# The second MLP pair with one tile per PSUM bank, two operand splits moved into the last w_in step, and even token groups

## The chip, the cores and the metric

The kernel runs on one core of one Trainium2 chip. The metric is the device time of one launch in microseconds (us), as the median of several runs. The profile comes from one further execution, taken with the hardware profiler; stretches below are given in us from that execution's first instruction.

## The reference

Linear attention per head, normalised by its root mean square, feeds two MLP pairs, all in float32:

```python
kv  = einsum('bhsd,bhse->bhde', k, v)             # 8 batches, 8 heads, 576 tokens, head size 64
out = einsum('bhsd,bhde->bhse', q, kv)
x   = out / sqrt(mean(out * out) + 1e-6) * g_norm  # turned to 4608 tokens x 512
x   = (sigmoid(x @ w_gate) * (x @ w_val)) @ w_out  # first pair, inner width 1536
h   = x @ w_in                                     # second pair, 512 -> 2048
g   = where(h >= 1, h, where(h <= -1, 0, (h + 1)**2 / 4))
y   = g @ w_out                                    # 2048 -> 512
```

The change touches the last three lines alone: the second pair.

## The kernel before, in words

Every float32 operand of a matmul is split into a high part, rounded to the type that the matrix engine takes (`fp32r`), and a low part, the remainder; a product is then three matmuls: high by high, high by low, low by high. ACT copies the high part and DVE subtracts to get the low one.

The second pair (`class Second`, from line 712) computes both matrix products with Winograd's form of Strassen's scheme: 2 x 2 blocks, seven products in place of eight, with sums taken before and after. The columns of a matmul are tokens. The 4608 tokens are cut into five groups. A group holds two halves of `n2` tokens each, with `n2` from `SIZES` (512, 512, 512, 384, 384), so that each matmul is 128 x 128 by `n2` columns.

A group has two stages, written out by hand in one function, `group` (line 810); each engine runs its own instructions in the order in which that function issues them.

- **w_in.** Eight steps `s`. A step forms seven products, each of six matmuls (`product`, line 774, matmuls on line 778), and so 42 matmuls. They go to four PSUM banks: `A` takes a11, later s2 and s3 on top; `D` takes a12; `B` takes s1, later s4 on top; `C` takes a22. Between the products ACT copies the state of a bank to SBUF (`p[:, 0]`, `p[:, 1]`, `u[:, 0]`, `u[:, 1]`, tiles named `kept`), and DVE adds bank and copy into the four quarters `q` of a tile `G[k]` (named `g`, two steps to a tile). Even steps use banks 0 to 3, odd steps 4 to 7. The activation `g` of the reference is a chain for two quarters at a time (`chain`, line 817): ACT relu (line 822), ACT square (line 825), DVE min and max (line 828). It runs a step late, as `late[0]` to `late[5]`, between the next step's copies and adds.
- **w_out.** 28 pieces `m`, seven products by four tiles `G[k]`, 12 matmuls each (line 910). A piece takes an operand that `split` (line 836) makes: ACT copies its high part, DVE the low part, into a tile named `gh` of the pool `gsp`, which has three buffers and which the tiles `r` of the chain share. `split(m + 2)` is issued ahead of the matmuls of piece `m`. After every fourth piece a result is copied out of a bank by ACT or added by DVE and, when complete, stored.

The weights of a step (`wst`, 1792 KB) and of an out product (`wo`, 2048 KB) come by DMA from DRAM on the SP queue, each with two buffers. SP runs its DMAs in order, a wait included.

Banks are allocated in pairs: `banks` (line 787) gives a tile of two banks, `A` and `D` are the halves of one such tile, `B` and `C` those of another. In w_out a result of two column blocks (`o` = 0, 1) fills the two halves of one tile. The tile framework keeps order by whole tiles: an instruction that writes a tile waits for those that read it, whichever half they touch.

Just ahead of the second pair, `store` (line 591) copies the first pair's last result out of PSUM to four SBUF tiles `ev` and sends them to DRAM by POOL's queue. The pools of the second pair take over the first pair's SBUF; a tile there waits until what lay in its place is done.

Of the kernel before, what the change touches and what calls it, by code (L numbers as in the profile page):

```python
# [7 lines left out]
F32 = mybir.dt.float32  # L8
# [3 lines left out]
ALU = mybir.AluOpType  # L12
# [2 lines left out]
NT, DM, FF1, FF2 = B * S, H * D, 1536, 2048  # L15
P = 128
T = 512
SIZES = (512, 512, 512, 384, 384)
NB = NT // T
NP = H // 2  # L20
KC = DM // P
# [12 lines left out]
def attn_gated_mlp_kernel(ctx: ExitStack, tc: tile.TileContext, a: dict, out: bass.AP):  # L34
# [33 lines left out]
    def act_copy(o, i):  # L68
        nc.scalar.activation(out=o, in_=i, func=AF.Copy)  # L69
# [4 lines left out]
    def split(src, hi, lo):  # L74

        act_copy(hi, src)
        nc.vector.tensor_tensor(out=lo, in0=src, in1=hi.bitcast(F32), op=ALU.subtract)  # L77
        return hi, lo
# [626 lines left out]
    class Second:  # L705
# [13 lines left out]
        def tt(self, o, x, y, op):  # L719
            nc.vector.tensor_tensor(out=o, in0=x, in1=y, op=op)  # L720
# [63 lines left out]
            t = self.wo2[i] = self.wo2p.tile([P, HF, 2, 2 * P], F32R, name="wo2", tag="wo2")  # L784
            nc.sync.dma_start(out=t.bitcast(F32), in_=wo2d[d][:, at])

        def banks(self, n):
            pool = (self.chain_p, self.acc_p)[n // 2]
            return pool.tile([P, 2, T], F32, name=f"bank{n}", tag=f"bank{n % 2}")[:, :, :self.n]

        def kept(self):
            return self.sv.tile([P, 2, T], F32, name="kept", tag="kept")[:, :, :self.n]
# [18 lines left out]
        def group(self, g, more):  # L811
# [25 lines left out]
            def split(m):  # L837
                i, k = divmod(m, HF // 2)
                src = G[k][:, self.OUT[i][1]]
                o = ops[m] = self.gsp.tile([P, 2, 2, T], F32R, name="gh2", tag="gsp")[:, :, :, :n2]  # L840
                act_copy(o[:, 0], src)
                tt(o[:, 1], src, o[:, 0].bitcast(F32), ALU.subtract)

            late = ()
            for s in range(HF):
                X, Y = (self.banks(s % 2 * 2 + e) for e in range(2))
                A, D, B, C = X[:, 0], X[:, 1], Y[:, 0], Y[:, 1]
                q = [G[s // 2][:, i, s % 2] for i in range(4)]
                self.ws = self.w_next
                if s + 1 < HF:  # L850
                    self.w_next = self.w_load(s + 1) if s else self.w_after
                elif more:
                    x = self.x_load(g + 1)
                if s in (2, 4):
                    self.wo2_load(s // 2 - 1)
                p, u = self.kept(), self.kept()
                r = self.gsp.tile([P, 4, T], F32, name="r", tag="gsp")[:, :, :n2]
                this = chain(s, 0, r[:, 0:2]) + chain(s, 2, r[:, 2:4])
                self.product(A, "a11", "b11")
                act_copy(p[:, 0], A)  # L860
                self.product(D, "a12", "b21")
                if late:
                    late[1]()
                tt(q[0], D, p[:, 0], ALU.add)
                self.product(B, "s1", "t1")
                act_copy(p[:, 1], B)
                if late:
                    late[3]()
                    late[2]()
                self.product(A, "s2", "t2", False)  # L870
                act_copy(u[:, 0], A)
                if late:
                    late[4]()
                self.product(C, "a22", "t4")
                if late:
                    late[5]()
                self.product(B, "s4", "b22", False)
                tt(q[1], B, u[:, 0], ALU.add)
                this[0]()
                if s and s % 2 == 0:  # L880
                    t1(s // 2 - 1)
                self.product(A, "s3", "t3", False)
                act_copy(u[:, 1], A)
                tt(q[2], A, p[:, 1], ALU.add)
                tt(q[3], C, u[:, 1], ALU.add)
                late = this
# [1 line left out]
            late[1]()  # L888
            late[3]()
            late[2]()  # L890
            split(0)
            late[4]()
            late[5]()
            split(1)
            t1(HF // 2 - 1)
            A, E, D, C = (self.banks(n) for n in range(4))
            bank = (A, E, A, D, E, A, C)
            if more:
                steps = self.x_steps(x)
# [5 lines left out]
            def matmuls(m, o):  # L905
                i, k = divmod(m, HF // 2)
                for e in range(2):
                    for n, (h, l) in enumerate(((0, 0), (0, 1), (1, 0))):
                        first = k == e == n == 0 and i in (0, 1, 3, 6)
                        nc.tensor.matmul(bank[i][:, o], self.wo2[i][:, 2 * k + e, h, o * P:(o + 1) * P], ops[m][:, l, e],  # L910
                                         start=first, stop=k == HF // 2 - 1 and e == 1 and n == 2, skip_group_check=True)

            for m in range(last + 1):
                i, k = divmod(m, HF // 2)
                if m + 2 <= last:
                    split(m + 2)
                if 2 <= m < 6:
                    tt(G[m - 2][:, 1], G[m - 2][:, 2], G[m - 2][:, 1], ALU.subtract)
                if 8 <= m < 12:
                    tt(G[m - 8][:, 0], G[m - 8][:, 1], G[m - 8][:, 0], ALU.subtract)  # L920
                if 12 <= m < 16:
                    tt(G[m - 12][:, 3], G[m - 12][:, 3], G[m - 12][:, 1], ALU.subtract)
                if more and (m in (0, 1, 6, 7) or 16 <= m < 24):
                    run(steps, 1)
                if more and m == 24:
                    self.w_after = self.w_load(1)
                if k == 0 and i + 1 < 7 and i:
                    self.wo2_load(i + 1)
                for o in range(2):
                    matmuls(m, o)  # L930
                    if m == last:
                        tt(u3[:, o], C[:, o], u3[:, o], ALU.add)
                        goes(1, 0, u3, slice(o, o + 1))
                if k == HF // 2 - 1:
                    if i == 0:
                        p1 = self.kept()
                        act_copy(p1, A)
                    elif i == 1:
                        p5 = self.kept()
                        act_copy(p5, E)  # L940
                    elif i == 2:
                        u2 = self.kept()
                        act_copy(u2, A)
                    elif i == 3:
                        tt(p1, D, p1, ALU.add)
                        goes(0, 0, p1)
                    elif i == 4:
                        tt(u2, E, u2, ALU.add)
                        goes(0, 1, u2)
                    elif i == 5:  # L950
                        u3 = self.kept()
                        act_copy(u3, A)
                        tt(p5, A, p5, ALU.add)
                        goes(1, 1, p5)


    with tc.manual_schedule():
# [368 lines left out]
        for k, j in enumerate(pairs):  # L1326
# [73 lines left out]
            if more:  # L1400
                run(steps)
                store(j + 1, norm_tags)
            else:
                run(second.xsteps)
                store(j + 1, ("nm", "nr", "nt", "wol"))
        first_part.close()
        second.rest()

# [39 lines left out]
```

## Time and profile before

| what | value |
|---|---|
| median of 3 runs | 1752.38 us (1751.16 to 1753.39) |
| the profiled execution | 1749.95 us, of which its span is 1748.0 us |
| granted TensorE clock, mean of the span | 0.984 |
| PE busy, share of the span | 95% |
| ACT, DVE busy | 52%, 67% |
| second pair, first to last matmul | from 952.4 us to about 1744.4 us |

Busy time of PE is the union of its matmuls' durations. A matmul's duration covers its way through the array, so that the next one starts well before it ends; the time per matmul is the distance from one start to the next. "Idle before" and the name behind the arrow say how long an engine had nothing to do and which instruction's end let it go on. PEclk is the granted share of the clock: 1.0 is 2.4 GHz, 0.5 is 1.2 GHz. In a table by stage the engines stand in the order PE, PEld (weight loads), DVE, ACT, POOL, each with its number of instructions in brackets.

### The profile page before, as it was taken

The numbers are of one execution on the slowest core, as the hardware profiler recorded it, in microseconds if no ns is written. First come the engines' busy times: TensorE is split into PE (matmuls) and PEld (weight loads), VectorE is DVE, ScalarE is ACT, GpSimd is POOL, SyncE is SP. The second block draws the span as 40 slices with busy tenths as digits, with TensorE's granted clock in tenths as the row PEclk, the third lists the DMA queues.
The fourth block names the chain that finished last, engine by engine and source line by source line (L and its number), as shares of the span: only waits on it lengthen the run. The fifth ranks groups of instructions, "written<-read, shape, count | busy, mean of one in ns | idle before, by whom it ended". The sixth has DMA issues, their size and how long they took to land.

```text
span 1748.0 us, 22357 instructions
## 1 busy us (share of the span) xinstructions
PE 1667.2 (95%) x8132; PEld 1378.3 (79%) x8132; DVE 1178.1 (67%) x1734; ACT 914.8 (52%) x1336; POOL 186.0 (11%) x292
## 2 busy tenths in 40 slices
PE   9999999999999999999998989998999899989888
PEld 6778887888878877888786767776877688888888
DVE  6888747768667678768745458745855685575565
ACT  4453445456477577544433565456536654553553
POOL 1212122323200111112211000000000000000000
PEclk8999999999999999999999999999999999999999
DMA  9776776677757778699855464555357445755825
GB/s 295 241 243 230 244 256 222 211 250 255 241 172 250 261 232 280 202 370 357 299 171 200 181 237 161 193 223 217 145 187 270 157 169 205 307 187 210 320 112 194
DMA packets 123678, 400.02 MB, mean 229 GB/s; under 512 B 15657, under 2 KB 22953, under 8 KB 113969
## 3 DMA queue, kind: packets, MB, share of 16 engines
q1 hardware_dynamic: 102640, 331.48, 54.7%
q0 software_dynamic: 20928, 67.13, 10.3%
q8 instruction: 64, 1.05, 0.2%
q14 instruction: 46, 0.37, 0.1%
HBM read 315.18 MB, written 83.36 MB: 228 GB/s over the span
## 4 chain that ended last, share of the span: by engine, by line
PE 79%; issue 7%; DMA 5%; ACT 4%; DVE 4%; POOL 1%; SPq 0%; POOLq 0%; DVEq 0%; ACTq 0%
PE bank L910 19%; PE bank L778 16%; PE h L94 6%; PE h L95 6%; PE h L96 6%; PE acc L94 5%; PE acc L95 4%; PE acc L96 4%; PE pA L648 4%; PE pE L648 3%; DMA wst<-w2d 2%; ACT kept L69 2%; DMA wo<-wo2d 1%; ACT r L822 1%; PE kvps L159 1%
## 5 line engine op out<-in xcount | busy, mean ns | idle before, releaser
L910 PE MATMUL bank<-gh,wo 128*128 128x512 f32 (+1 forms) x1680 | 363.6, 377 | 33.0 <-ACT gh L69 21.9
L910 PEld LDWEIGHTS bank<-gh,wo 128*128 128x128 f32 x1680 | 314.7, 194 | 81.9 <-ACT gh L69 27.3
L69 ACT ACTIVATE gh<-g 128x1024 fp32r<-128x1024 f32 (+2 forms) x164 | 151.4, 923 | 158.6 <-PE bank L910 132.2
L778 PE MATMUL bank<-x_t,wst 128*128 128x512 f32 (+1 forms) x960 | 210.8, 368 | 0.0
L778 PE MATMUL bank<-x_b,wst 128*128 128x512 f32 (+1 forms) x720 | 174.1, 377 | 35.6 <-ACT kept L69 33.2
L720 DVE TENSOR_TENSOR gh<-g,gh 128x1024 fp32r<-128x1024 f32 (+1 forms) x140 | 156.2, 1116 | 55.8 <-ACT gh L69 54.7
L778 PEld LDWEIGHTS bank<-x_t,wst 128*128 128x128 f32 x960 | 175.9, 188 | 22.7
L69 ACT ACTIVATE kept<-bank 128x512 f32<-128x512 f32 (+3 forms) x180 | 106.4, 591 | 166.7 <-PE bank L778 131.5
L720 DVE TENSOR_TENSOR g<-bank,kept 128x512 f32<-128x512 f32 (+1 forms) x160 | 98.1, 634 | 135.9 <-PE bank L778 87.0
L778 PEld LDWEIGHTS bank<-x_b,wst 128*128 128x128 f32 x720 | 129.4, 189 | 68.3 <-ACT kept L69 48.5
L94 PE MATMUL acc<-gh,woh 128*128 128x512 f32 x420 | 164.8, 392 | 0.0
L95 PE MATMUL acc<-gl,woh 128*128 128x512 f32 x420 | 163.8, 390 | 0.3 <-DVE gl L77 0.3
L94 PE MATMUL h<-xh,w 128*128 128x512 f32 x384 | 151.6, 395 | 0.0
L95 PE MATMUL h<-xl,w 128*128 128x512 f32 x384 | 149.7, 390 | 0.2 <-DVE xl L84 0.2
L96 PE MATMUL h<-xh,w 128*128 128x512 f32 x384 | 149.5, 389 | 0.0
L828 DVE SCALAR_TENSOR_TENSOR g<-r,g 128x1024 f32<-128x1024 f32 (+1 forms) x80 | 89.1, 1114 | 82.2 <-ACT r L825 82.2
L96 PE MATMUL acc<-gh,woh 128*128 128x512 f32 x324 | 126.2, 389 | 0.0
L822 ACT ACTIVATE r<-g,half 128x1024 f32<-128x1024 f32 (+1 forms) x80 | 85.0, 1062 | 76.0 <-DVE g L720 76.0
L648 PE MATMUL pA<-xc,wc 128*128 128x512 f32 x432 | 111.1, 393 | 3.1 <-ACT u L69 3.0
L648 PEld LDWEIGHTS pA<-xc,wc 128*128 128x128 f32 x432 | 81.3, 189 | 21.2 <-ACT u L69 4.3
L94 PEld LDWEIGHTS acc<-gh,woh 128*128 128x128 f32 x420 | 78.8, 188 | 18.7 <-issue 1.2
L95 PEld LDWEIGHTS acc<-gl,woh 128*128 128x128 f32 x420 | 78.8, 188 | 17.2 <-DVE gl L77 1.1
(193 smaller groups left out, 2655.2 us busy)
## 6 DMA issues: line engine op xcount, KB each, us to landing
wst<-w2d SPq DMA_DIRECT2D x40, 1792.0 KB, 7.5
wo<-wo2d SPq DMA_DIRECT2D x35, 2048.0 KB, 8.1
wc<-w1d SPq DMA_DIRECT2D x168, 256.0 KB, 5.4
woh<-wo1d SPq DMA_DIRECT2D x162, 256.0 KB, 4.8
raw<-in_w SPq DMA_DIRECT2D x32, 512.0 KB, 5.7
raw<-in_w_gv SPq DMA_DIRECT2D x24, 512.0 KB, 5.5
w1d<-w2half POOLq DMA_DIRECT2D x48, 256.0 KB, 4.2
w2d<-w2half POOLq DMA_DIRECT2D x48, 256.0 KB, 4.8
```

Source lines behind the costliest of these rows:

```text
L69: nc.scalar.activation(out=o, in_=i, func=AF.Copy)
L94: nc.tensor.matmul(ps, w[0][:, wsl], x[0], start=first, stop=False)
L95: nc.tensor.matmul(ps, w[0][:, wsl], x[1], start=False, stop=False)
L96: nc.tensor.matmul(ps, w[1][:, wsl], x[0], start=False, stop=last)
L159: nc.tensor.matmul(ps[g * D:(g + 1) * D, e], k[:, s], v[:, s], start=c == 0, stop=c == NSC)
L648: nc.tensor.matmul(o, w[:, h, sl], x[c][l], start=first and c == n == 0, stop=c == 1 and n == 2, skip_group_check=True)
L720: nc.vector.tensor_tensor(out=o, in0=x, in1=y, op=op)
L778: nc.tensor.matmul(bank, self.ws[w][h][:, sl], self.xo[x][:, l, c], start=first and c == n == 0, stop=c == 1 and n == 2, skip_group_check= ...
L822: nc.scalar.activation(out=r, in_=v, func=AF.Relu, bias=self.half, scale=0.5)
L828: nc.vector.scalar_tensor_tensor(out=v, in0=r, scalar=1.0, in1=v, op0=ALU.min, op1=ALU.max)
L910: nc.tensor.matmul(bank[i][:, o], self.wo2[i][:, 2 * k + e, h, o * P:(o + 1) * P], ops[m][:, l, e], start=first, stop=k == HF // 2 - 1 and ...
```

## The change

Five edits, all for the second pair.

1. `SIZES` becomes (464, 464, 464, 464, 448). The number of matmuls and the sum of their columns stay what they were.
2. `bank` replaces `banks`: eight tiles of one bank each.
3. In the last w_in step, `split(0)` is issued behind `late[4]` and `split(1)` behind the relu `this[0]`; they were issued behind the step, between `late[2]`, `late[4]` and `late[5]`.
4. In w_out a result that was copied by one ACT instruction over two banks, or added by one DVE instruction, takes two, one per bank (`keep`, `result`).
5. The first pair's last `store` takes its four `ev` tiles from the pool of the weights (`wo`) in place of four tiles of the pool of temporaries.

```diff
-SIZES = (512, 512, 512, 384, 384)
+SIZES = (464, 464, 464, 464, 448)
...
-        def banks(self, n):
-            pool = (self.chain_p, self.acc_p)[n // 2]
-            return pool.tile([P, 2, T], F32, name=f"bank{n}", tag=f"bank{n % 2}")[:, :, :self.n]
+        def bank(self, n):
+            pool = (self.chain_p, self.acc_p)[n // 4]
+            return pool.tile([P, T], F32, name=f"bank{n}", tag=f"bank{n % 4}")[:, :self.n]
...
-                X, Y = (self.banks(s % 2 * 2 + e) for e in range(2))
-                A, D, B, C = X[:, 0], X[:, 1], Y[:, 0], Y[:, 1]
+                A, D, B, C = (self.bank(s % 2 * 4 + e) for e in range(4))
...
                 if late:
                     late[4]()
+                if s == HF - 1:
+                    split(0)
                 self.product(C, "a22", "t4")
...
                 this[0]()
+                if s == HF - 1:
+                    split(1)
...
             late[2]()
-            split(0)
             late[4]()
             late[5]()
-            split(1)
             t1(HF // 2 - 1)
-            A, E, D, C = (self.banks(n) for n in range(4))
+            A, E, D, C = ([self.bank(n + o) for o in range(2)] for n in (0, 2, 4, 6))
...
+            def keep(b):
+                t = self.kept()
+                for o in range(2):
+                    act_copy(t[:, o], b[o])
+                return t
+
+            def result(h, e, b, t):
+                for o in range(2):
+                    tt(t[:, o], b[o], t[:, o], ALU.add)
+                goes(h, e, t)
...
                     if m == last:
-                        tt(u3[:, o], C[:, o], u3[:, o], ALU.add)
+                        tt(u3[:, o], C[o], u3[:, o], ALU.add)
...
                 run(second.xsteps)
-                store(j + 1, ("nm", "nr", "nt", "wol"))
+                store(j + 1, None)
```

How the instructions move is read from the built programs. First PE, the third w_in step of the first group; a row is an instruction, out<-in, columns, and the semaphores that it waits for (`Activation` is ACT). `x_b_9359` is the operand of the product into `D`. Before:

```order
L778 MATMUL bank_9696<-x_b_9323,wst 128x512 [waits DMAHW5_49]
L778 MATMUL bank_9696<-x_b_9323,wst 128x512 x5
L778 MATMUL bank_9696<-x_b_9359,wst 128x512 [waits Activation_49]
L778 MATMUL bank_9696<-x_b_9359,wst 128x512 x5
L778 MATMUL bank_9697<-x_t_9382,wst 128x512 x6
L778 MATMUL bank_9696<-x_t_9424,wst 128x512 [waits DVE_49]
L778 MATMUL bank_9696<-x_t_9424,wst 128x512 x5
L778 MATMUL bank_9697<-x_t_9460,wst 128x512 [waits Activation_49]
L778 MATMUL bank_9697<-x_t_9460,wst 128x512 x5
L778 MATMUL bank_9697<-x_b_9479,wst 128x512 x6
L778 MATMUL bank_9696<-x_t_9513,wst 128x512 [waits Activation_49]
L778 MATMUL bank_9696<-x_t_9513,wst 128x512 x5
```

and now:

```order
L778 MATMUL bank_9700<-x_b_9323,wst 128x464 [waits DMAHW5_49,DVE_49]
L778 MATMUL bank_9700<-x_b_9323,wst 128x464 x5
L778 MATMUL bank_9701<-x_b_9359,wst 128x464 x6
L778 MATMUL bank_9702<-x_t_9382,wst 128x464 x6
L778 MATMUL bank_9700<-x_t_9424,wst 128x464 [waits Activation_49]
L778 MATMUL bank_9700<-x_t_9424,wst 128x464 x5
L778 MATMUL bank_9703<-x_t_9460,wst 128x464 [waits DVE_49]
L778 MATMUL bank_9703<-x_t_9460,wst 128x464 x5
L778 MATMUL bank_9702<-x_b_9479,wst 128x464 [waits Activation_49]
L778 MATMUL bank_9702<-x_b_9479,wst 128x464 x5
L778 MATMUL bank_9700<-x_t_9513,wst 128x464 [waits Activation_49]
L778 MATMUL bank_9700<-x_t_9513,wst 128x464 x5
```

The first matmul into `D` (operand `x_b_9359`) waited for ACT, which reads `A`; now it waits for nothing, and the waits that are left stand where a product is added on top of a bank.

Second ACT, from the last w_in step of the first group into w_out. `r<-g` is the relu, `r<-r` the square, `kept<-bank` the copy of a bank, `gh_...<-g_...` the high part of a split. Before:

```order
L69 ACTIVATE kept<-bank_10018 128x512 [waits DVE_49,PE_49]
L825 ACTIVATE r<-r 128x1024 [waits Activation_49]
L822 ACTIVATE r<-g_9576,half_9571 128x1024 [waits DVE_49]
L69 ACTIVATE kept<-bank_10018 128x512 [waits PE_49]
L825 ACTIVATE r<-r 128x1024 [waits Activation_49]
L822 ACTIVATE r<-g_9576,half_9571 128x1024 [waits DVE_49]
L69 ACTIVATE gh_10087<-g_9573 128x1024
L825 ACTIVATE r<-r 128x1024 [waits Activation_49]
L69 ACTIVATE gh_10092<-g_9574 128x1024
L69 ACTIVATE gh_10102<-g_9575 128x1024 [waits DVE_49]
```

and now:

```order
L69 ACTIVATE kept<-bank_10032 128x464 [waits PE_49]
L825 ACTIVATE r<-r 128x2x464 [waits Activation_49]
L69 ACTIVATE gh_10078<-g_9573 128x2x464
L822 ACTIVATE r<-g_9576,half_9571 128x2x464 [waits DVE_49]
L69 ACTIVATE gh_10096<-g_9574 128x2x464 [waits Activation_49]
L69 ACTIVATE kept<-bank_10032 128x464 [waits PE_49]
L825 ACTIVATE r<-r 128x2x464 [waits Activation_49]
L822 ACTIVATE r<-g_9576,half_9571 128x2x464 [waits DVE_49]
L825 ACTIVATE r<-r 128x2x464 [waits Activation_49]
L69 ACTIVATE gh_10124<-g_9575 128x2x464 [waits PE_49]
L69 ACTIVATE x_b_10127<-xin 128x2x464 [waits DMAHW6_49,DMAHW5_49]
L69 ACTIVATE gh_10142<-g_9576 128x2x464 [waits DVE_49,PE_49]
```

The first two `gh` copies have moved up: the first stands ahead of the last step's first relu, the second ahead of its last copy of a bank. The third `gh` copy now waits for PE, because the buffer that it gets is the first one's.

Third DVE at the same place. `g<-bank,kept` adds a bank and its copy, `g<-r,g` is the min and max, `gh<-g,gh` the low part of a split. Before:

```order
L828 SCALAR_TENSOR_TENSOR g_9576<-r,g_9576 128x2x512 [waits DVE_49,Activation_49] x2
L720 TENSOR_TENSOR g_9576<-bank_10019,kept 128x512 [waits PE_49]
L720 TENSOR_TENSOR g_9576<-bank_10018,kept 128x512 [waits Activation_49]
L720 TENSOR_TENSOR g_9576<-bank_10019,kept 128x512
L828 SCALAR_TENSOR_TENSOR g_9576<-r,g_9576 128x2x512 [waits DVE_49,Activation_49]
L720 TENSOR_TENSOR gh_10087<-g_9573,gh_10087 128x1024 [waits Activation_49]
L828 SCALAR_TENSOR_TENSOR g_9576<-r,g_9576 128x2x512 [waits DVE_49,Activation_49]
L720 TENSOR_TENSOR gh_10092<-g_9574,gh_10092 128x1024 [waits DMASW6_49,DMASW7_49,DMASW5_49,Activation_49]
L720 TENSOR_TENSOR g_9576<-g_9576 128x1024 [waits DVE_49]
L720 TENSOR_TENSOR gh_10102<-g_9575,gh_10102 128x1024 [waits DMASW1_49,DMASW2_49,DMASW0_49,Activation_49]
```

and now:

```order
L720 TENSOR_TENSOR g_9576<-bank_10033,kept 128x464 [waits PE_49,Activation_49]
L828 SCALAR_TENSOR_TENSOR g_9576<-r,g_9576 128x2x464 [waits DVE_49,Activation_49]
L720 TENSOR_TENSOR gh_10078<-g_9573,gh_10078 128x2x464 [waits Activation_49]
L828 SCALAR_TENSOR_TENSOR g_9576<-r,g_9576 128x2x464 [waits DVE_49]
L720 TENSOR_TENSOR g_9576<-bank_10034,kept 128x464 [waits PE_49]
L720 TENSOR_TENSOR gh_10096<-g_9574,gh_10096 128x2x464 [waits DMASW6_49,DMASW5_49,DMASW7_49,DVE_49,Activation_49]
L720 TENSOR_TENSOR g_9576<-bank_10032,kept 128x464 [waits Activation_49]
L720 TENSOR_TENSOR g_9576<-bank_10035,kept 128x464
L828 SCALAR_TENSOR_TENSOR g_9576<-r,g_9576 128x2x464 [waits DVE_49,Activation_49] x2
L720 TENSOR_TENSOR g_9576<-g_9576 128x2x464 [waits DVE_49]
L720 TENSOR_TENSOR gh_10124<-g_9575,gh_10124 128x2x464 [waits Activation_49]
```

The first low part now stands ahead of a min and max and of the add `g<-bank_10034`, and the second ahead of the last two adds.

## Rows read from the trace of the kernel before

**Rows 1.** Busy time by stage: stretch and length, then engines' busy us, PEclk, DMA share, GB/s

```profile
952.40:1045.20 92.80, 80.03 (x337) 63.32 (x335) 40.16 (x49) 46.56 (x61) 2.26 (x5) 0.96 0.60 218
...
1131.10:1215.20 84.10, 78.56 (x337) 62.28 (x336) 40.06 (x48) 45.78 (x60) 0.00 (x0) 1.00 0.57 210
1215.20:1220.10 4.90, 0.21 (x1) 0.00 (x0) 2.44 (x4) 4.49 (x6) 0.00 (x0) 0.74 0.76 255
1220.10:1300.00 79.90, 78.64 (x337) 64.18 (x338) 66.05 (x57) 39.99 (x39) 0.00 (x0) 0.97 0.49 185
...
1470.00:1537.40 67.40, 61.52 (x337) 57.86 (x335) 31.52 (x48) 36.31 (x60) 0.00 (x0) 1.00 0.66 254
...
1541.40:1607.80 66.40, 62.49 (x337) 61.05 (x338) 51.16 (x57) 31.54 (x39) 0.00 (x0) 0.95 0.59 220
```

**Rows 2.** Who PE waited for, 952 to 1748 us: total us, times, longest

```profile
PE bank L778 <- ACT kept L69: 33.2, 40, 8.0
PE bank L910 <- ACT gh L69: 21.9, 5, 4.7
PE bank L910 <- DMA wo<-wo2d: 4.7, 5, 1.5
PE bank L910 <- DVE kept L720: 3.7, 5, 0.8
...
PE bank L778 <- DMA wst<-w2d: 2.4, 4, 0.9
```

**Rows 3.** Timeline, a w_in step at 512 columns: start us, length us, engine, instruction

```profile
1164.30 0.60 ACT L69 ACTIVATE kept<-bank 128x512 f32<-128x512 f32 x1 [0.20 <-PE bank L778]
...
1164.95 1.65 PE L778 MATMUL bank<-x_b,wst 128*128 128x512 f32 x6 [0.69 <-ACT kept L69]
...
1166.45 4.24 PE L778 MATMUL bank<-x_t,wst 128*128 128x512 f32 x18
...
1170.53 1.52 PE L778 MATMUL bank<-x_b,wst 128*128 128x512 f32 x6
```

**Rows 4.** Timeline, PE alone, a w_in step at 384 columns

```profile
1500.90 1.20 PE L778 MATMUL bank<-x_b,wst 128*128 128x384 f32 x6
1501.94 1.21 PE L778 MATMUL bank<-x_t,wst 128*128 128x384 f32 x6
```

**Rows 5.** Timeline, the first w_in step of all

```profile
961.24 0.60 ACT L69 ACTIVATE kept<-bank 128x512 f32<-128x512 f32 x1 [8.04 <-DMA x2d<-ev]
...
961.89 2.93 PE L778 MATMUL bank<-x_b,wst 128*128 128x512 f32 x6 [7.97 <-ACT kept L69]
```

**Rows 6.** Timeline, the handover from w_in to w_out, second group

```profile
1214.97 1.15 ACT L822 ACTIVATE r<-g,half 128x1024 f32<-128x1024 f32 x1 [1.90 <-DVE g L720]
...
1216.03 0.58 ACT L69 ACTIVATE kept<-bank 128x512 f32<-128x512 f32 x1
...
1216.64 1.29 DVE L720 TENSOR_TENSOR g<-bank,kept 128x512 f32<-128x512 f32 x2 [1.70 <-ACT kept L69]
...
1217.96 1.15 ACT L822 ACTIVATE r<-g,half 128x1024 f32<-128x1024 f32 x1 [0.41 <-DVE g L720]
1219.02 1.04 ACT L69 ACTIVATE gh<-g 128x1024 fp32r<-128x1024 f32 x1
...
1220.09 1.23 DVE L720 TENSOR_TENSOR gh<-g,gh 128x1024 fp32r<-128x1024 f32 x1 [1.03 <-ACT gh L69]
...
1220.11 0.79 PE L910 MATMUL bank<-gh,wo 128*128 128x512 f32 x1 [4.70 <-ACT gh L69]
...
1221.37 23.88 PE L910 MATMUL bank<-gh,wo 128*128 128x512 f32 x98 [0.47 <-DVE gh L720]
```

**Rows 7.** Instruction groups by shape, PE, line 186: busy us, mean ns

```profile
L186 PE MATMUL X<-qraw,kvw 64*64 64x512 f32 x16 | 4.1, 614 | 0.1
...
L186 PE MATMUL X<-qraw,kvw 64*64 64x448 f32 x16 | 2.9, 562 | 0.0
```

**Rows 8.** DMA issues, 1494 to 1503 us: size, us from issue to landing

```profile
wst<-w2d SPq DMA_DIRECT2D x1, 1792.0 KB, 9.1
```

More of the change, by code (lines that the diff above doesn't have):

```diff
@@ L909, in matmuls @@
                         first = k == e == n == 0 and i in (0, 1, 3, 6)
-                        nc.tensor.matmul(bank[i][:, o], self.wo2[i][:, 2 * k + e, h, o * P:(o + 1) * P], ops[m][:, l, e],
+                        nc.tensor.matmul(bank[i][o], self.wo2[i][:, 2 * k + e, h, o * P:(o + 1) * P], ops[m][:, l, e],
                                          start=first, stop=k == HF // 2 - 1 and e == 1 and n == 2, skip_group_check=True)
+            def keep(b):
[7 more added lines that the diff above has]
+                goes(h, e, t)
             for m in range(last + 1):
@@ L935, in group @@
                     if i == 0:
-                        p1 = self.kept()
-                        act_copy(p1, A)
+                        p1 = keep(A)
                     elif i == 1:
-                        p5 = self.kept()
-                        act_copy(p5, E)
+                        p5 = keep(E)
                     elif i == 2:
-                        u2 = self.kept()
-                        act_copy(u2, A)
+                        u2 = keep(A)
                     elif i == 3:
-                        tt(p1, D, p1, ALU.add)
-                        goes(0, 0, p1)
+                        result(0, 0, D, p1)
                     elif i == 4:
-                        tt(u2, E, u2, ALU.add)
-                        goes(0, 1, u2)
+                        result(0, 1, E, u2)
                     elif i == 5:
[L951 to L954, printed above, removed]
+                        u3 = keep(A)
+                        result(1, 1, A, p5)
     with tc.manual_schedule():
```

## The prediction

> **What bounds the kernel now.** The first view to read is busy time by stage [rows 1]: it gives how long each stage of the second pair takes, which is to be held against its matmuls alone. The price of a matmul is in the timelines. At 512 columns 18 of them run from 1166.45 to 1170.53 [rows 3], 0.2267 us each; at 384 columns six run from 1500.90 to 1501.94 [rows 4], 0.1733 us each. The difference, 0.0533 us for 128 columns, is 2.4 columns per ns. A stage has 336 matmuls: 76.2 us at 512, 58.2 us at 384. Six wide stages and four narrow ones are 690 us; from 952.4 to about 1744.4 the second pair takes 792. So 102 us are not matmul time, and they are what the change can touch. [Rows 1] place them: a wide w_in takes 84.1 (7.9 over), its handover to w_out 4.9, its w_out 79.9 (3.7 over). A narrow w_in is 9.2 over, a narrow w_out 8.2. The first w_in takes 92.8, 8.7 more than the second.
>
> Who is waited for is the second view [rows 2]: 40 waits for the ACT copy `kept`, one a step; five for ACT's `gh`, one a handover; then DMAs and DVE.
>
> **The waits in w_in.** [Rows 3] show the 40 waits: ACT copies bank A at 1164.30, and the product into bank D starts at 1164.95, after 0.69 us idle. The copy reads A, the product writes D; they share a tile. With what the restart costs, a wide step loses 7.9 / 8 = 0.99 us, a narrow one a little less. The order of the changed program has no wait on that product. What is late next: the product on top of A waits for the same copy, but two products later, 2.5 us, and the copy takes 0.6 us. ACT's work in a step, four copies, two relus and two squares (0.6 and about 1.1 us, [rows 6]), is under 7 us of the 8.7 that a step will take, and DVE's less. So I take this wait as gone at full: nothing else in the step is late by the rows.
>
> The first step's wait is another one [rows 5]: `kept` lies where the last `ev` tiles lay, and its copy stands 8.04 us until their DMA has landed; PE stands 7.97. With `ev` in the weights' pool that place is under `wo`, which is first loaded two steps later. I keep 0.5 us of 8.7.
>
> **The sizes.** By the price per column, 464 columns cost 0.1733 + 80 / 2400 = 0.2067 us and 448 cost 0.2000. A step is 8.68 us, a piece of w_out 2.48, and the ten stages are 690 us as before: the sizes by themselves give nothing. The nearest rows that show widths off the 128 grid are those of line 186 [rows 7]: 448 columns take 562 ns and 512 take 614, so 64 columns fewer are paid back, though in another data format. If 464 cost what 512 does, the ten stages would take 72 us more.
>
> What the sizes do change is the time that a DMA has. A `wst` load beside a `wo` load took 9.1 us [rows 8]; a step is 8.68. In the narrow groups PE waited 2.4 us for `wst` and, mostly there, 4.7 for `wo` [rows 2]: about 3.6 a group at most. At 512 next to nothing is left of it. 464 lies 3/8 of the way from 512 to 384, which gives 1.3; I take 1.5 a group, 7.5 in all, since PE now comes to each step without the old wait. The bounds are 0 and 3.6 a group.
>
> The Trainium skill ("DMA: Bandwidth & Descriptors", Specifications) puts a core's share of the HBM at about 358 GB/s. A w_in stage will move eight `wst`, two `wo` and one group's input, some 21 MB by the sizes of the DMAs, in 69.5 us: 300 GB/s. By that rule the sum stays as it is; the narrow w_in of [rows 1] ran at 254 GB/s, so no run yet shows 300 held over a stage.
>
> **The handover.** Two splits are moved here, and the queues that they are moved into decide. [Rows 6] give the old chain at 512: the relu of the last step's first half at 1214.97, the copy of bank A at 1216.03, two DVE adds from 1216.64, the second relu at 1217.96, `gh` at 1219.02, and PE's first matmul at 1220.11, 4.9 us after the end of w_in at 1215.2. The second matmul needs the low part (DVE, 1.23 us) and starts at 1221.37.
>
> Now let E be the end of w_in, at 464 columns, and let every ACT and DVE time be 0.91 of its row's. `gh` and `gl` of pieces 0 and 1 have been moved into the queues of the last step, which are in order. The first `gl` stands ahead of a min and max and of the add that releases the relu, and it waits for the first `gh`, which waits behind a square. The relu, at E - 0.2 without it, is later by one copy and one subtraction, 0.95 + 1.05: E + 1.8. Then the second `gh` runs to E + 3.8, and the second `gl` to E + 4.9, ahead of the last two adds (1.2): E + 6.1. Second relu to E + 7.0, square to E + 8.0, third `gh` to E + 9.0. On DVE a min and max, a sum and the third `gl` follow the square, 3.2: E + 11.3.
>
> The wait that the third `gh` has on PE, with an input split and the fourth `gh` behind it on ACT, is for piece 0, done by E + 2.7, and costs nothing.
>
> PE: piece 0 starts at once and ends at E + 2.7. Piece 1 has its first matmul at E + 3.8, its second, with the low part, at E + 4.95, and ends at E + 7.2. Piece 2 has its first at E + 9.0, its second at E + 11.3, and ends at E + 13.6; piece 3 ends at E + 16.1. Without waits it would be 4 x 2.48 = 9.9. So 6.2 us are lost: two stalls in place of one.
>
> To this comes the clock. In a wide w_out stretch PEclk is 0.97 [rows 1]: 0.03 x 79.9 / 0.5 = 4.8 us at 1.2 GHz, just behind PE's long idle time, which cost 2.4. In the narrow one it is 0.95: 6.6 us, cost 3.3. After the change PE idles 2 us and then nearly 4, less at a stretch than the 4.9 before. The bounds are 0 and 3.3; I take 2.0, near what the rows show. A handover then costs 8.2, and five cost 41. Before, the wait, the second matmul's and the clock cost 4.9 + 3.7 less the 0.8 of the stage's last wait, 7.8 in a wide group. The change gains nothing here.
>
> [...]
>
> **The rest.** In w_out the last block waits for DVE's read of the other half of C, 3.7 us in five [rows 2]: two tiles now, so gone. The seven copies and adds of a group that become two halves each are on ACT and DVE, which have 39.99 and 66.05 us of 79.9 to do there [rows 1]. Two copies of 512 take 2 x 0.58 and one operation of twice the width 1.04 [rows 6], so a split adds 0.1 us; it is hidden, and without that cover it would be 3.5 us in all. Six more input DMAs (pieces that cross a tile of 512 tokens) stand on SP in the last step; behind them are the next group's first weights, due a whole w_out later. The last store is 448 wide and not 384: 0.2 us.
>
> **Sum.** Left over the matmuls: 0.5 + 41 + 7.5 + 0.2 = 49 of 102, so 53 us go: about 39 from the waits in w_in, 8 at the start, 4 at the ends of w_out, 2 from narrow DMA waits. The profiled execution took 1749.95, and so 1697; the median of the runs lies 2.4 higher. Forecast: 1700.
>
> **Rivals.**
> *The handover shrinks.* If the first `gl` does not hold up the add (because ACT gets to the first `gh` earlier than I place it), the relu stays at E - 0.2, the chain reaches the third `gl` some 3.2 earlier, and no stall is long enough for the clock: about 3 us a handover, 26 less in all, 1674. For it: ACT has idle time in a step. Against: the square in front of `gh` ends only when DVE wants to go on.
> *The weights set the pace.* If every `wst` takes the 9.1 of [rows 8], a step is 9.3 with the issue, not 8.68: 40 x 0.62 = 25, of which 2 are counted: 1722. For it: that row. Against: it is one beside a `wo` load, and six of eight steps have none.
> *Slower: the odd width.* If a matmul of 464 or 448 columns costs what 512 does, 3360 of them cost 72 us more: 1772. It decides from 53 / 3360 = 0.016 us a matmul. For it: no row shows 464 in this format. Against: [rows 7] and the exact 2.4 columns per ns between 384 and 512.
> That the new tiles keep the old wait can be left out, since the order shows it gone.
>
> **How the numbers follow.** Forecast 0.72, its own range 1688 to 1712: the clock's bounds are 10 down and 6.5 up, those of the DMA waits 7.5 down and 10.5 up, and they hardly all fall on one side. Handover shrinks 0.12; weights 0.12; odd width 0.04. The range, 1680 to 1722, takes in half of the first and most of the second rival. A measurement can tell 0.2%, 3.5 us, from no change. Faster: all but the last rival and a remainder, 0.95; within 0.2%: 0.01; slower: 0.04.
>
> **What would show it.** In the changed profile: no idle time in front of the second product of a step; a w_in step of 8.7 us; matmul starts 0.207 us apart; the first w_in no longer than the second; in each w_out two stalls, one in piece 1 and a longer one in piece 2, with the third `gh` 9 us and its `gl` 11 us behind the end of w_in. I am wrong if w_out runs through, if `wst` ends the waits in most steps, or if the matmuls lie 0.227 apart.

## The result and the profile after

The changed kernel takes 1706.26 us (median of four runs, 1705.52 to 1708.1), the kernel before 1751.77 beside it (1749.75 to 1753.39). The ratio is 0.9742, interval 0.9725 to 0.9759: 45.5 us less, with 1700 forecast. The profiled run is the slowest of the four, 1708.1 us with a span of 1706.1. Its second pair begins 4.7 us later than before's, at 957.1; 4.3 of these were there 20 us after the program's start, in code that the change doesn't touch. So stages are compared by their lengths: the second pair took 792 us and takes 745.1 (957.13 to 1702.20), 46.9 less.

Busy time by stage in the changed kernel, with the columns of [rows 1]: the first group's w_in and w_out, the second group's, the fourth's w_out, the last group's two stages.

```profile
957.13:1027.68 70.55, 70.55 (x337) 62.95 (x336) 36.10 (x48) 43.54 (x61) 2.26 (x5) 1.00 0.75 284
1027.68:1107.60 79.92, 74.42 (x337) 64.65 (x336) 63.78 (x65) 40.56 (x47) 0.00 (x0) 0.96 0.53 195
1107.60:1178.80 71.20, 70.94 (x337) 62.80 (x336) 36.22 (x48) 42.92 (x60) 0.00 (x0) 1.00 0.65 248
1178.80:1257.64 78.84, 74.83 (x338) 64.97 (x337) 63.67 (x65) 40.55 (x47) 0.00 (x0) 0.96 0.53 199
1478.10:1557.90 79.80, 74.18 (x338) 64.81 (x337) 63.39 (x65) 40.38 (x47) 0.00 (x0) 0.96 0.53 196
1557.90:1625.99 68.09, 68.09 (x337) 63.05 (x336) 35.12 (x48) 41.75 (x60) 0.00 (x0) 1.00 0.58 231
1625.99:1702.20 76.21, 70.81 (x337) 63.63 (x335) 50.88 (x54) 33.59 (x40) 0.00 (x0) 0.98 0.42 156
```

PE is busy through the whole of a w_in: 70.55 of 70.55 us in the first group, where [rows 1] had 80.03 of 92.8. The first group's w_in is no longer than the second's. What is still lost stands in w_out: 79.92 us for 336 matmuls. Who PE waits for from the second pair's start on, with the columns of [rows 2] (line 911 is w_out's matmul here, as line 910 was before):

```profile
PE bank L911 <- DVE gh L720: 12.6, 10, 1.9
PE bank L911 <- ACT gh L69: 7.8, 7, 1.5
PE bank L911 <- DMA wo<-wo2d: 4.0, 5, 1.9
PE bank L778 <- DMA wst<-w2d: 0.5, 2, 0.3
```

The 40 waits for `kept` on line 778 are gone, and so are the five of w_out's end. For the two parts of `gh` there were ten waits, five for the high part [rows 2] and five short ones for the low part, which DVE makes:

```profile
PE bank L910 <- DVE gh L720: 2.5, 5, 0.7
```

Now there are 17, ten of them for the low part; in all they take 20.4 us and took 24.4.

The timeline of a w_in step, which answers to [rows 3 to 5]: start, length, engine, instruction.

```profile
1125.24 2.68 PE L778 MATMUL bank<-x_b,wst 128*128 128x464 f32 x12
...
1126.70 0.56 ACT L69 ACTIVATE kept<-bank 128x464 f32<-128x464 f32 x1 [0.21 <-PE bank L778]
...
1127.76 3.94 PE L778 MATMUL bank<-x_t,wst 128*128 128x464 f32 x18
...
1131.54 1.42 PE L778 MATMUL bank<-x_b,wst 128*128 128x464 f32 x6
```

The first two products of the step are one piece, 12 matmuls without a gap, while ACT still copies bank A. And 18 matmuls start in 1131.54 - 1127.76 = 3.78 us: 0.2100 each, not the 0.2067 of the forecast.

The timeline of the first group's handover answers to [rows 6]. w_in ends at E = 1027.68.

```profile
1025.57 0.98 ACT L69 ACTIVATE gh<-g 128x928 fp32r<-128x928 f32 x1
...
1026.57 1.12 DVE L720 TENSOR_TENSOR gh<-g,gh 128x928 fp32r<-128x928 f32 x1 [3.25 <-ACT gh L69]
...
1027.62 1.12 DVE L828 SCALAR_TENSOR_TENSOR g<-r,g 128x928 f32<-128x928 f32 x1
1027.68 2.68 PE L911 MATMUL bank<-gh,wo 128*128 128x464 f32 x12
...
1028.65 0.63 DVE L720 TENSOR_TENSOR g<-bank,kept 128x464 f32<-128x464 f32 x1
1029.32 1.07 ACT L822 ACTIVATE r<-g,half 128x928 f32<-128x928 f32 x1 [2.78 <-DVE g L720]
1030.30 0.96 ACT L69 ACTIVATE gh<-g 128x928 fp32r<-128x928 f32 x1
...
1031.31 0.47 PE L911 MATMUL bank<-gh,wo 128*128 128x464 f32 x1 [0.94 <-ACT gh L69]
...
1032.46 2.57 PE L911 MATMUL bank<-gh,wo 128*128 128x464 f32 x11 [0.69 <-DVE gh L720]
...
1035.54 0.96 ACT L69 ACTIVATE gh<-g 128x928 fp32r<-128x928 f32 x1
...
1036.55 0.47 PE L911 MATMUL bank<-gh,wo 128*128 128x464 f32 x1 [1.52 <-ACT gh L69]
...
1038.91 13.46 PE L911 MATMUL bank<-gh,wo 128*128 128x464 f32 x51 [1.89 <-DVE gh L720]
```

Piece 0 starts at once, as it should; then PE stands before pieces 1 and 2, for the high part and for the low part of each. DVE's first low part stands 3.25 us in its queue for `gh` (1026.57), with a min and max and then the add of bank B behind it (1028.65), and the relu waits 2.78 us for that add (1029.32).

### The profile page after: what moved, and what is told of

It reads as the page before. It is cut to its first block, busy times and chain, and to the rows that moved or that the text cites. A ratio compares the mean times of both kernels' runs of the same rounds, so it can differ in the third digit from the quotient of the medians.

```text
span 1706.1 us, 22387 instructions
## 1 busy us (share of the span) xinstructions
PE 1668.4 (98%) x8132; PEld 1400.4 (82%) x8132; DVE 1179.4 (69%) x1749; ACT 916.3 (54%) x1356; POOL 186.3 (11%) x292
## 5 line engine op out<-in xcount | busy, mean ns | idle before, releaser
L911 PE MATMUL bank<-gh,wo 128*128 128x464 f32 (+1 forms) x1680 | 369.9, 381 | 24.6 <-DVE gh L720 12.6
L911 PEld LDWEIGHTS bank<-gh,wo 128*128 128x128 f32 x1680 | 323.1, 193 | 70.6 <-DVE gh L720 15.5
L69 ACT ACTIVATE gh<-g 128x928 fp32r<-128x928 f32 (+2 forms) x164 | 150.6, 922 | 158.3 <-PE bank L911 133.9
L778 PE MATMUL bank<-x_t,wst 128*128 128x464 f32 (+1 forms) x960 | 212.9, 370 | 0.0
L720 DVE TENSOR_TENSOR gh<-g,gh 128x928 fp32r<-128x928 f32 (+1 forms) x140 | 156.1, 1116 | 73.6 <-ACT gh L69 72.8
L69 ACT ACTIVATE kept<-bank 128x464 f32<-128x464 f32 (+1 forms) x200 | 110.0, 550 | 109.4 <-PE bank L778 91.5
L778 PE MATMUL bank<-x_b,wst 128*128 128x464 f32 (+1 forms) x720 | 163.3, 371 | 0.6 <-DMA wst<-w2d 0.5
L720 DVE TENSOR_TENSOR g<-bank,kept 128x464 f32<-128x464 f32 (+1 forms) x160 | 98.0, 633 | 83.7 <-PE bank L778 43.7
L828 DVE SCALAR_TENSOR_TENSOR g<-r,g 128x928 f32<-128x928 f32 (+1 forms) x80 | 89.0, 1113 | 76.5 <-ACT r L825 76.5
L822 ACT ACTIVATE r<-g,half 128x928 f32<-128x928 f32 (+1 forms) x80 | 85.0, 1063 | 84.2 <-DVE g L720 84.2
```

What stands on the lines that cost most here:

```text
L778: nc.tensor.matmul(bank, self.ws[w][h][:, sl], self.xo[x][:, l, c], start=first and c == n == 0, stop=c == 1 and n == 2, skip_group_check= ...
L822: nc.scalar.activation(out=r, in_=v, func=AF.Relu, bias=self.half, scale=0.5)
L828: nc.vector.scalar_tensor_tensor(out=v, in0=r, scalar=1.0, in1=v, op0=ALU.min, op1=ALU.max)
L911: nc.tensor.matmul(bank[i][o], self.wo2[i][:, 2 * k + e, h, o * P:(o + 1) * P], ops[m][:, l, e], start=first, stop=k == HF // 2 - 1 and e ...
```

## Experiments

A table first, for the second pair alone: its length from the first to the last matmul start, and what is left over when matmul time at the straight-line price (n / 2400 + 0.0136 us, 690.6 us in every row) is taken off; this holds every wait, slow matmul and dear width. The last column is what a handover loses from the end of w_in through the fifth piece of w_out, against matmuls at the stage's own measured price, as the smallest and largest of the five groups.

| kernel | time, us | second pair | left over | a handover costs |
|---|---|---|---|---|
| before | 1751.77 | 791.8 | 101.1 | 7.3 to 8.8 |
| changed | 1706.26 | 744.9 | 54.3 | 6.0 to 8.7 |
| sizes as before | 1707.56 | 747.9 | 57.2 | 5.6 to 9.5 |
| splits as before | 1706.92 | 745.2 | 54.6 | 7.3 to 8.1 |
| splits rearranged | 1680.17 | 720.0 | 29.4 | 0.8 to 2.5 |
| banks alone | 1714.53 | 755.0 | 64.4 | 7.0 to 8.4 |
| `ev` place alone | 1744.74 | 783.9 | 93.2 | 6.5 to 8.7 |
| rearranged further | 1667.91 | 706.8 | 16.2 | 0.3 to 0.4 |

**The sizes undone.** The theory was that the sizes by themselves are worth little.

```diff
-SIZES = (464, 464, 464, 464, 448)
+SIZES = (512, 512, 512, 384, 384)
```

> The changed kernel with the old group sizes (512, 512, 512, 384, 384). Theory: 464 and 448 columns cost about 3 ns a matmul more than the straight line between 384 and 512, some 10 us in 3360 matmuls, but the old narrow groups would now wait for their weights, since a step of 42 x 0.1733 = 7.28 us is shorter than a load of 1792 KB takes (7.4 to 9.1 us): about 7 us a narrow w_in and 3 to 4 a narrow w_out, 20 in all. So the second pair takes some 752 us against 745 in the changed kernel, and the run some 1713. Rival: the even sizes cost more than they give back; then the second pair takes 735 to 740 us and the run is below 1702.

Measured: 1707.56 us (1706.81 to 1708.53), ratio to before 0.974, interval 0.9722 to 0.9759. The second pair is 747.9 us, 3.0 longer than in the changed kernel, between the two expectations. The two last rows of PE's waits here stand against 0.5 and 4.0 of the changed kernel:

```profile
PE bank L778 <- DMA wst<-w2d: 7.0, 7, 1.7
PE bank L911 <- DMA wo<-wo2d: 5.6, 4, 2.8
```

Outside the handovers some 11 us more are lost, nearly all in the narrow groups, which wait for their weights (restarts included); in return 512 and 384 columns cost their 0.2267 and 0.1733 again. Two effects of about 10 us cancel: the weights' time, of which the forecast had a part, and the dearer width, which it did not have.

**The splits undone.** The banks, the sizes and the `ev` place stay; the two splits go back behind the last step's relu and behind its end.

```diff
                 if late:
                     late[4]()
-                if s == HF - 1:
-                    split(0)
...
-                if s == HF - 1:
-                    split(1)
...
             late[2]()
+            split(0)
             late[4]()
             late[5]()
+            split(1)
```

> The changed kernel with the two splits where they stood before, behind the last w_in step. Theory: a handover loses as much either way, 7.8 us against 7.7, because the splits that were moved up hold up the adds behind them: the run stays within 4 us of 1706. Its w_out then has one stall of some 4.6 us ahead of piece 0 and runs through from piece 1. Rival: the move is worth what the long stall was, and undoing it costs 4 us or more a handover, 20 in all: 1726.

Measured: 1706.92 us (1703.48 to 1709.8), ratio 0.9737 (0.9716 to 0.9757), second pair 745.2 us: the same as with the splits moved. The stall is one again, in front of piece 0, as in [rows 6]:

```profile
PE bank L909 <- ACT gh L69: 21.5, 5, 4.3
```

So the moved splits are worth nothing, as the forecast had it: they exchange one stall of 4.3 us, with slow matmuls behind it, for two pairs of shorter ones.

**The splits rearranged.** If the chain is late because DVE stands in its queue for the first `gh`, with the add behind it, places at which nothing has to be waited for must give the gain that the move was to bring. Here `gh` and its low part are issued apart. The first copy moves up once more, behind the previous step's first square, and its low part behind the first of that step's two min and max; in DVE's queue it still stands ahead of the add of bank B. The second copy goes behind the step's last copy of a bank, its low part behind the last adds; the third and fourth split go among the last chain's instructions, ahead of w_out.

```diff
                 act_copy(o[:, 0], src)
+                yield
                 tt(o[:, 1], src, o[:, 0].bitcast(F32), ALU.subtract)
...
+            def high(m):
+                parts[m] = split(m)
+                next(parts[m])
+
+            def low(m):
+                run(parts.pop(m))
...
                 if late:
                     late[1]()
+                if s == HF - 1:
+                    high(0)
...
                     late[2]()
+                if s == HF - 1:
+                    low(0)
...
-                if s == HF - 1:
-                    split(0)
...
-                if s == HF - 1:
-                    split(1)
...
                 act_copy(u[:, 1], A)
+                if s == HF - 1:
+                    high(1)
...
             late[1]()
+            low(1)
             late[3]()
+            high(2)
             late[2]()
+            low(2)
             late[4]()
             late[5]()
+            high(3)
+            low(3)
...
-                if m + 2 <= last:
-                    split(m + 2)
+                if 4 <= m + 2 <= last:
+                    high(m + 2)
+                    low(m + 2)
```

> The changed kernel with the first four splits laid where ACT and DVE have nothing due, the high and the low part apart: the first high part behind the square of late[1] and its low part behind the min and max of late[2], the second behind the last copy of a bank and the last adds, the third and fourth between the last chain's instructions. Nothing is left out. Theory: the stalls come from the order in the queues, so the adds and the relu go on as if there were no split; piece 1's second matmul is then about 1 us late, pieces 2 and 3 at most 0.5, and the clock does not fall: 1 to 2 us a handover, 30 us less than the changed kernel in all, a run of some 1676. Rival: piece 2 must wait for the activation chain whatever the order; then 5 us or more stay at each handover and the run is above 1690.

Measured: 1680.17 us (1675.26 to 1682.03), ratio 0.958 (0.9558 to 0.9603), second pair 720.0; nearer the theory's 1676 than the rival's 1690. PE's waits in the second pair (line 927 is w_out's matmul):

```profile
PE bank L927 <- DVE gh L720: 8.2, 9, 1.3
PE bank L927 <- DMA wo<-wo2d: 3.9, 5, 1.9
PE bank L778 <- DMA wst<-w2d: 1.3, 2, 1.0
PE bank L778 <- DVE g L720: 0.6, 1, 0.6
```

No wait for ACT's `gh` is left. In the first group, whose w_in ends at 1028.63 here, the copy is early, DVE makes the low part without standing for it (1024.19), and the relu starts 0.26 us ahead of w_in's end, where in the changed kernel it started 1.64 behind:

```profile
1022.60 0.97 ACT L69 ACTIVATE gh<-g 128x928 fp32r<-128x928 f32 x1
...
1024.19 1.12 DVE L720 TENSOR_TENSOR gh<-g,gh 128x928 fp32r<-128x928 f32 x1
...
1028.37 1.07 ACT L822 ACTIVATE r<-g,half 128x928 f32<-128x928 f32 x1 [1.74 <-DVE g L720]
```

The handover's loss was the order in two queues: 28 of the 38.5 us that five handovers cost come back without a faster instruction, and the second pair gets 25 shorter. The other 3 go to waits in w_in and to 448 columns, which cost 0.2067 and 0.2040 here. Part of the 28 is the clock. PE still stands twice in the second group's w_out, and the clock stays at 1.00:

```profile
1172.28:1245.97 73.69, 71.18 (x338) 62.73 (x336) 61.91 (x62) 40.11 (x47) 0.00 (x0) 1.00 0.57 212
```

```profile
1175.86 7.82 PE L927 MATMUL bank<-gh,wo 128*128 128x464 f32 x36 [0.70 <-DVE gh L720]
1184.93 5.28 PE L927 MATMUL bank<-gh,wo 128*128 128x464 f32 x24 [1.25 <-DVE gh L720]
```

**Five widths.** What a matmul costs between 384 and 512 columns, in the changed kernel.

```diff
-SIZES = (464, 464, 464, 464, 448)
+SIZES = (496, 480, 464, 448, 416)
```

> The changed kernel with the groups 496, 480, 464, 448 and 416 columns wide, the same sum, to read the price of a matmul from the distance of starts in each stage. A straight line through 384 (0.1733 us) and 512 (0.2267) gives 0.2200, 0.2133, 0.2067, 0.2000, 0.1867. Theory: every width off a multiple of 128 pays some 3 ns on top: 0.223, 0.2165, 0.2097, 0.2027, 0.190. Rival one: 464 is dear for its own number (it is no multiple of 32 or 64), and 480, 448 and 416 lie within 1 ns of the line. Rival two: the price has nothing to do with the width but with how far ACT and DVE run beside, and then it differs between w_in and w_out of one group.

Measured: 1714.01 us in the one run. The mean distance of two starts, by group, w_in and w_out (starts over 30 ns late left out), against the straight line:

| columns | by the line | w_in | w_out |
|---|---|---|---|
| 496 | 0.2200 | 0.2200 | 0.2231 |
| 480 | 0.2133 | 0.2167 | 0.2166 |
| 464 | 0.2067 | 0.2094 | 0.2100 |
| 448 | 0.2000 | 0.2057 | 0.2065 |
| 416 | 0.1867 | 0.1881 | 0.1878 |

Every one of these widths but 496 in w_in is dearer than the line, by 1.1 to 6.5 ns. So neither expectation holds whole: the 3 ns of the theory fit 480 and 464, but 448 pays twice that and 416 less than half; 464 is not alone in being dear (first rival); and the price differs clearly between w_in and w_out of one group only at 496 (second rival). In the trace of the 480 group one sees it in the starts: 18 matmuls in 1121.74 - 1117.84 = 3.90 us, 0.2167 each.

```profile
1117.84 4.06 PE L778 MATMUL bank<-x_t,wst 128*128 128x480 f32 x18
1121.74 1.46 PE L778 MATMUL bank<-x_b,wst 128*128 128x480 f32 x6
```

**The banks alone.** The kernel before with one-bank tiles and the result blocks in halves; sizes, splits and the `ev` place as they were.

```diff
-                X, Y = (self.banks(s % 2 * 2 + e) for e in range(2))
-                A, D, B, C = X[:, 0], X[:, 1], Y[:, 0], Y[:, 1]
+                A, D, B, C = (self.bank(s % 2 * 4 + e) for e in range(4))
...
-            A, E, D, C = (self.banks(n) for n in range(4))
+            A, E, D, C = ([self.bank(n + o) for o in range(2)] for n in (0, 2, 4, 6))
...
```

> The kernel before, with one change: each PSUM bank a tile of its own, and the copies and adds of w_out's result blocks made in halves. Sizes (512, 512, 512, 384, 384), the splits and the place of the `ev` tiles stay. Theory (the old wait in w_in was a wait on the shared tile): the 40 waits in front of the second product go, 24 of 0.98 us and 16 of 0.85, together 37 us, and so do the five at the ends of w_out, 5 us; the two narrow groups wait longer for their weights, as in the run with the old sizes, by 7 us; the first step's wait of 8 us stays. Together 35 us: 1717, with 1712 to 1722. Rival (the sizes or the place of `ev` carry a part of it, since a step that comes sooner then meets DMA or ACT): 20 us or less, 1732 or more, and the wait in front of the second product is still there under another releaser.

Measured: 1714.53 us (1713.19 to 1715.77) against 1751.39 beside it, ratio 0.979 (0.9774 to 0.9805), within the theory's range; the left-over falls by 36.7 us. PE's waits:

```profile
PE bank L909 <- ACT gh L69: 22.0, 5, 4.7
PE bank L778 <- DMA wst<-w2d: 7.1, 6, 1.7
PE bank L778 <- ACT kept L69: 5.6, 1, 5.6
PE bank L909 <- DMA wo<-wo2d: 5.3, 3, 2.8
```

One wait for `kept` stays, of 5.6 us: the first step's, now in front of the next product into A and not in front of the one into D. The narrow groups wait 7.1 us for `wst` where they waited 2.4 [rows 2]. The banks are the change's main part.

**The `ev` place alone.**

```diff
-                store(j + 1, ("nm", "nr", "nt", "wol"))
+                store(j + 1, None)
```

> The kernel before, with one change: the last `ev` tiles lie in the weights' pool. Theory: the first step's wait for the copy `kept` shrinks from 8 us to about that of the other steps, so 7 to 8.5 us less: 1744 to 1745. Rival (whatever is loaded first then waits for the same DMA): 0 to 3 us, with the 8 us in front of the first wst or wo operand.

Measured: 1744.74 us (1741.53 to 1752.12), ratio 0.9963 (0.9948 to 0.9978), 6.7 us less by the medians; left-over 7.9 us less in the profiled execution. The waits for `kept` are 40 still, with a longest of 0.7 us, where [rows 2] have 8.0:

```profile
PE bank L778 <- ACT kept L69: 26.0, 40, 0.7
```

The two edits alone add up to 36.7 + 7.9 = 44.6 us of left-over, and both together, with the sizes as before and the splits moved (which gave nothing), took off 101.1 - 57.2 = 43.9: they don't meet.

**The rest of the handover.** On the rearranged splits, the next group's first input steps go where DVE has time, and each piece takes its four products with the high part first.

```diff
-                if more and (m in (0, 1, 6, 7) or 16 <= m < 24):
+                if more and (4 <= m < 8 or 16 <= m < 24):
...
-                for e in range(2):
-                    for n, (h, l) in enumerate(((0, 0), (0, 1), (1, 0))):
+                for n, (h, l) in enumerate(((0, 0), (1, 0), (0, 1))):
+                    for e in range(2):
```

> The order of e3_splits_new with two further edits: the first four input steps of the next group stand at pieces 4 to 7 of w_out and not at 0, 1, 6 and 7, and a piece multiplies both high operand halves with both weight parts before it takes the low ones (four matmuls that need only the copy, and not one). What was left at a handover in e3 was 0.94 us in piece 1, for the low part, and 1.5 us in piece 4, behind DVE's input steps. Theory: piece 4's wait goes at full (4 x 1.5) and piece 1's to 0.3 or less (5 x 0.65): 9 us under e3, 1671, with 1667 to 1675. Rival (PE then meets the next product of the chain, ACT's third or fourth `gh`, or the input steps pushed later hold up a split there): 1676 to 1681, no gain, with the wait in piece 2, 3 or 8.

Measured: 1667.91 us (1665.48 to 1668.8), ratio 0.952 (0.9504 to 0.9535); second pair 706.8. One wait by name is left in it, and a w_out (the second row's stretch) is 71.54 us at full clock where the changed kernel took 79.92 at 0.96:

```profile
PE bank L927 <- DMA wo<-wo2d: 2.8, 5, 1.2
```

```profile
955.54:1026.12 70.58, 70.58 (x337) 62.87 (x336) 37.70 (x49) 43.81 (x62) 2.26 (x5) 1.00 0.76 284
1026.12:1097.66 71.54, 71.20 (x338) 62.69 (x336) 61.44 (x62) 40.24 (x47) 0.00 (x0) 1.00 0.59 218
```

This version beats both kernels, the changed one by 38 us. Against the splits rearranged the second pair is 13.2 us shorter; 9.0 of it are the handovers, as the theory had it, and the rest fewer waits for DMAs and 448 columns at 0.2027 again, which it had not. What each of the two edits gave was not run. Of the 16.2 us left, some 9 are the dearer widths.

**448 without 464.** Whether the dearer price follows the width, on the rearranged splits.

```diff
-SIZES = (464, 464, 464, 464, 448)
+SIZES = (512, 512, 448, 448, 384)
```

> The order of e3_splits_new with the sizes (512, 512, 448, 448, 384), so that no stage is 464 wide. What is asked is the price of a matmul: by the line through 384 and 512 it is 0.2267, 0.2000 and 0.1733; 448 has shown 0.2027 in the changed kernel and 0.2057 in the run with five widths. If the extra belongs to the width, 448 lies at 0.203 to 0.207 in all four stages; if it belonged to the change of width from stage to stage, 448 comes to 0.200 in the second of its groups. The time by the line is that of e3, 1680; with 4 x 336 matmuls of 448 at 0.0027 to 0.0067 more than the line and 384's DMA waits of 10 us or so: less 9 for e3's own extra, 1685 to 1690.

Measured: 1679.06 us in the one run, below the range expected: the expectation took the 384 group's DMA waits as coming on top of those of the other groups, but the two 512 groups have none. By group, 448 costs 0.2036 and 0.2052, then 0.2027 and 0.2057; 512 and 384 cost 0.2267 and 0.1734 in w_in. A step of each, 18 starts in 4.08 us (0.2267) and in 3.64 (0.2022):

```profile
984.69 4.24 PE L778 MATMUL bank<-x_t,wst 128*128 128x512 f32 x18
988.77 1.52 PE L778 MATMUL bank<-x_b,wst 128*128 128x512 f32 x6
```

```profile
1434.03 3.81 PE L778 MATMUL bank<-x_t,wst 128*128 128x448 f32 x18
1437.67 1.38 PE L778 MATMUL bank<-x_b,wst 128*128 128x448 f32 x6
```

The extra belongs to the width, in every group that has it, though not with one size: over the runs its stages have means from 0.2027 to 0.2067. What sets which one is open; nothing here was run that tells it.

## Why the prediction was right, and where it was off

**The waits in w_in: right.** Removed alone, the shared tiles took 36.7 us of left-over with them, and that is after 5.3 us more of PE's waits for DMAs (7.1 and 5.3 us against 2.4 and 4.7 [rows 2]); the five ends of w_out are in it too. Nothing else in the step was late: PE is busy throughout w_in, but for 0.5 us of waits for `wst`.

**The start: right.** 8.2 forecast; by itself the edit gave 7.9 in the profiled execution and 6.7 by the medians.

**The sizes: the mechanism right, a term mis-sized.** "A step is 8.68 us ... and the ten stages are 690 us as before" failed. At 464 columns a matmul costs 0.2097 us in the mean, not 0.2067, and at 448 it costs 0.2027, not 0.2000: 2688 x 0.0030 + 672 x 0.0027 = 9.9 us, so the ten stages are 700, and a step of w_in is 8.82 us (70.55 / 8). The forecast had joined two measured points on the grid by a line and read between them; the row of another format that it leaned on [rows 7] could not show 3 ns. This is more than what was missing in the second pair: 739 forecast, 745.1 measured, since what is left over the true matmul time is 745.1 - 700 = 45 us and not 49. Of those 4 us some 2.5 are the handovers and the rest the start and the weights; that they fell the other way is luck, no argument of the forecast. The slower rival was this same effect at full size; it has 3 of the 20 ns that it needed for 72 us.

**The handover: right, in its places too.** The forecast had PE's four restarts at E + 3.8, 4.95, 9.0 and 11.3; the trace has 3.63, 4.78, 8.87 and 11.23. Against matmuls that run on at 0.21, these four starts are 1.1, 0.9, 1.8 and 2.2 us late, 6.0 together (6.2 forecast), and slow matmuls behind them cost 2.6 (2.0), 8.6 with it; five handovers cost 38.5 (41 forecast, 8.2 each). The rival in which ACT reaches the first `gh` early needed the relu at E - 0.2; it is at E + 1.64, behind the add that the low part holds up. Its mechanism was sound all the same: with the splits rearranged the copy is early, the relu is at E - 0.26, and the run takes 1680, where the rival had 1674. The clock took its part: each w_out stretch above is at 0.96 or 0.98, and in the last version, without the stalls, at 1.00. The forecast's upper bound for the clock, 3.3 us and so 9.5 a handover, was not reached, 8.7 being the dearest. The Trainium skill ("TensorE: Matmul & The Clock Gate", HAM oscillation) tells of a kernel in which a wait for a DMA, longer than the matmuls between two such waits, brings the low clock each time. The waits here are of another kind, 0.7 to 1.9 us beside 70 us of matmuls: in the changed kernel the clock fell behind them at all five handovers, and with the splits rearranged it did not fall, with waits of 0.70 and 1.25 us.

**The weights: right.** 7.5 forecast for DMA waits, some 6 measured, 4.5 of them as PE's waits by name. The rival in which each `wst` takes 9.1 us is out: over the whole execution a `wst` takes 7.5 us in the median from issue to landing (first row), and from 1125 to 1136 us two of them, with a `wo` load between, take 7.0 (the two other rows).

```profile
wst<-w2d SPq DMA_DIRECT2D x40, 1792.0 KB, 7.5
```

```profile
wst<-w2d SPq DMA_DIRECT2D x2, 1792.0 KB, 7.0
wo<-wo2d SPq DMA_DIRECT2D x1, 2048.0 KB, 11.5
```

The `wo` load beside them takes 11.5 us, which is nothing new (12.6 in the kernel before, the median from 1470 to 1537 us); all waits of PE for `wo` are 4.0 us. The first w_in held 284 GB/s over 70 us with PE busy throughout, near the 300 that the forecast asked of it.

**What stays open.** Why widths between 384 and 512 cost extra. In the 464 stages starts alternate between 205 and 215 ns in most steps and lie at 207 to 210 in others; only the mean, about 210, is steady.

## What to carry over

Two banks in one tile cost a wait each time one is read while the other is to be written; a tile for each took 37 us off here, with sizes, splits and the `ev` place as they were. When an operation is moved earlier in an in-order queue, write down what it waits for there and what then stands behind it: two moved splits gave nothing while DVE stood 3.25 us for the first copy, and the first four gave 26 us at places where what they need is done in time. And take the price of a size from a row at that size; between two measured sizes a straight line was off by 1.4%, which over 3360 matmuls was more than the whole error in the second pair.

## What the runs showed of the hardware

- At full clock, matmuls in this format start 0.2267 us apart at 512 columns and 0.1734 at 384 (w_in of "448 without 464", late starts left out), which is n / 2.4 GHz + 13.4 ns. At 416, 448, 464 and 480 they start 1.1 to 6.7 ns further apart than that line; 496 cost nothing extra in w_in, 3.1 ns in w_out.
- In the changed kernel the granted clock of a w_out was 0.96 with stalls of 0.94, 0.69, 1.52 and 1.89 us behind its start, where one stall of 4.7 had gone with 0.97. With the splits rearranged it was 1.00 with stalls of 0.70 and 1.25 us, and in the last version 1.00 with 0.34 us of idle time in the stretch.
